# A second short GpSimd store ahead of the copies of zeros, and the copies cut 2, 9 and 4 instead of 11 and 4

## The chip, the core and the metric

The kernel runs on one core of one Trainium2 chip. The metric is the device time of one execution in microseconds; before the change it is 284.01 us, the median of four runs (283.77 to 284.34).

## What is computed

One decode step (one token for each of 4 batches) through a layer norm, attention over the last 1024 positions of a 4096 position cache, and a gelu-gated feed-forward block; then all gradients for a given `grad_out`. Cut to what matters here:

```python
def _A_ref(x, k_cache, v_cache, wq, wo):
    W = min(4096, max(256, Sk // 4))                       # 1024 of Sk = 4096
    k = jnp.repeat(k_cache[:, :, Sk - W:, :], rep, axis=1)
    v = jnp.repeat(v_cache[:, :, Sk - W:, :], rep, axis=1)
    ...
_out, _vjp = jax.vjp(_f, A_x, A_k_cache, A_v_cache, A_wq, A_wo, B_w_gate, B_w_up, B_w_down)
_grads = _vjp(grad_out)
```

The gradients of the two caches (`out_2` for K, `out_3` for V) have shape 4 x 8 x 4096 x 128 in bfloat16. Only the last 1024 of the 4096 rows of each head carry values. The first K0 = 3072 rows are zero, and must be written all the same: 2 x 4 x 8 x 3072 x 256 bytes, some 50 MB of the 81 MB that the kernel writes.

## The kernel before

The work goes through four steps `t` of two kv heads each; a feed-forward part stands in front. TensorE transposes and multiplies, VectorE and ScalarE take the results out of PSUM into staging tiles, and SyncE (SP) sends these to memory in the program's order. The stores of zeros are laid between these by hand: `zero()` (L161) sends two heads of one batch, 1536 KB, from the tile `ztile` as 128 pieces of 12288 bytes.

An execution's memory traffic is carried out by 16 DMA engines (not to be confused with the five compute engines). Each works through its share of every transfer, packet by packet, in the order of its queue; SP's transfers are one queue (q1), GpSimd's another (q0), ScalarE's a third (q10). In the trace each packet is a record with start, duration, size and queue, without the number of its engine. The end of an engine's share is a packet of 4 bytes, a completion mark.

`zero_15()` (L166) is called once, in the last step, and treats four heads of `out_3` in its own way. Head 3 is one store of SP (128 rows of 6144 bytes). For heads 0 to 2, GpSimd (POOL) copies from zeros that already lie in `out_2[0]`, memory to memory:

- L183, first, a short store: 5 rows of 16 positions each, that is 5 pieces of 4096 bytes from `ztile` to head 0.
- L184 to L186, two copies. With KR = K0 / 16 = 192, a "row" is 192 positions, 49152 bytes, for each of the 3 heads. The first copy has 11 such rows (33 pieces), the second 4 (12 pieces): 45 pieces, 15 x 192 = 2880 of the 3072 positions of each head.
- L187 and L188: what is left of heads 0 to 2 (192 positions less the 80 of the short store for head 0) goes out as three stores of 16 rows by SP, at the very end of the program, after head 3.

Each store is `store()` (L99, its transfer on L103), which also tells the scheduler that stores write disjoint parts. The order on each engine is that of the program. `zero_15()` is called after the products of the last softmax gradient are issued; on POOL its transfers stand behind the last two multiplications of L487.

Of the kernel before, what the change touches and what calls it, by code (L numbers as in the profile page):

```python
# [18 lines left out]
def kernel(  # L19
# [28 lines left out]
    nc = tc.nc  # L48
# [7 lines left out]
    K0 = Sk - W  # L56
# [43 lines left out]
    def store(eng, out, in_, kind):  # L100

        eng.nop()
        d = eng.dma_start(out=out, in_=in_)  # L103
        for k in ("rest", "zeros") if kind == "rest" else ("rest",):
            tc.declare_no_dep(d.ins, group=k, reason="stores write disjoint parts of the outputs")
        tc.add_to_no_dep_group(kind, d.ins)
        return d
# [58 lines left out]
    def zero_15():  # L166


        last = [z for z in zlist if z[0] is out_3][-2:]
        for z in last:  # L170
            zlist.remove(z)
        b, g = last[0][1:]
        assert last[1][1:] == (b, g + ZR)
        dst = out_3[b, g:g + 2 * ZR]
        KR = K0 // 16
        k0 = 15 * KR
        used = [80, 0, 0]

        def rest(eng, n, h, k0, w):
            src = ztile[0:8 * n - 7:8] if n < 16 else ztile[0:n]  # L180
            store(eng, dst[h, k0:k0 + n * w, :].rearrange("(m j) d -> m (j d)", m=n), src[:, 0:w * Dh], "zeros")

        rest(nc.gpsimd, 5, 0, k0, 16)  # L183
        for n, r in ((11, 0), (4, 11)):  # L184
            s_, d_ = (x[0:3, r * KR:(r + n) * KR, :].rearrange("g (m j) d -> m g (j d)", m=n) for x in (out_2[0], dst))
            store(nc.gpsimd, d_, s_, "zeros")  # L186
        return [lambda: rest(nc.sync, P, 3, 0, K0 // P)] + [  # L187
            lambda h=h: rest(nc.sync, 16, h, k0 + used[h], (KR - used[h]) // 16) for h in range(3)]  # L188


    nc.gpsimd.memset(ztile[:], 0.0)
# [512 lines left out]
    for f4 in range(NF4):  # L704
        held = {}
        n = min(4, NF - 4 * f4)
# [34 lines left out]
    with tc.tile_pool(name="kv_b", bufs=GP, reuse_waits="tile") as kv_b, \  # L741
# [7 lines left out]
        for t in range(NT):  # L749
# [13 lines left out]
            if t == NT - 1:  # L763
                rest = zero_15()
# [81 lines left out]
```

## Time and profile before

| | us |
|---|---|
| median of four runs | 284.01 |
| the profiled execution | 283.98 |
| its span in the trace | 282.2 |
| PE, DVE, ACT busy | 203.2, 164.4, 118.0 |
| POOL busy | 42.0 |
| last PE instruction ends | 255.6 |
| last DVE instruction ends | 260.6 |
| the three POOL transfers of `zero_15()` are issued | 224.37, 224.95, 225.57 |
| SP's last five transfers are issued | 265.82 to 271.38 |
| last packet on a DMA engine ends | 280.22 |

All times within the trace count from the start of the span. A row of the stretches view gives, for each stretch of time, the busy time of the engines, the granted clock of TensorE, the mean busy share of the 16 DMA engines and the rate that they moved. A row of the timeline gives start, duration, engine, line and what was moved.

### The profile page before, as it was taken

To read this page: it belongs to the slowest core of one execution; us is meant where nothing else is said; L and a number is where in the kernel's file an instruction comes from. 1 tells how busy PE (TensorE), PEld (TensorE's weight loads), DVE (VectorE), ACT (ScalarE), POOL (GpSimd) and SP (SyncE) were. 2 spreads that over 40 slices of the span, in tenths; PEclk is the share of its full clock that TensorE was granted. 3 is DMA by queue.
4 is the path that set the end of the run, shared out by engine and by line. 5 is a ranking of instruction groups with operands and counts; after the bars stand their busy time and mean duration, and the time that the engine had idled before them with its cause. 6 is when DMAs were issued, how large, how long until landed. Compare 5 with 4: busy or idle time off the path is not lost.

```text
span 282.2 us, 6863 instructions
## 1 busy us (share of the span) xinstructions
PE 203.2 (72%) x2962; PEld 139.5 (49%) x2972; DVE 164.4 (58%) x313; ACT 118.0 (42%) x219; POOL 42.0 (15%) x43
## 2 busy tenths in 40 slices
PE   0276699959789889998999199898999599272000
PEld 0265476735456675556765056676555474031000
DVE  7946646645776555577666158767677638178000
ACT  2030386635035418753547155453866048160000
POOL 8600000007002250002340000232000600000000
PEclk9999589986999999999999869999999979958555
DMA  7999999999999999999999999999999999999991
GB/s 269 392 376 432 429 423 419 428 422 419 368 398 425 410 409 420 425 403 422 423 413 414 420 428 422 423 387 410 380 370 413 398 383 377 411 428 426 412 419 44
DMA packets 19677, 112.12 MB, mean 397 GB/s; under 512 B 1806, under 2 KB 4654, under 8 KB 11411
## 3 DMA queue, kind: packets, MB, share of 16 engines
q1 hardware_dynamic: 17696, 101.33, 87.5%
q0 software_dynamic: 1792, 8.52, 7.7%
q10 hardware_dynamic: 160, 1.84, 1.8%
q8 instruction: 23, 0.38, 0.5%
q14 instruction: 6, 0.05, 0.0%
HBM read 32.89 MB, written 81.01 MB: 404 GB/s over the span
## 4 chain that ended last, share of the span: by engine, by line
PE 47%; DMA 23%; DVE 15%; ACT 3%; issue 2%; SPq 0%; DVEq 0%; ACTq 0%
DMA out_dram<-stg_dv 13%; PE T_ps L303 8%; PE kv_ps L508 6%; DMA wd_sb<-in_B_w_down_dram 6%; PE S_ps L369 5%; PE od_ps L474 5%; DMA out_dram<-osb_g 4%; DVE T_sb L98 3%; PE dwq_ps L544 2%; DVE dS_s L391 2%; PE wdT_ps L303 2%; PE acc_ps L280 2%; PE wgT_ps L303 2%; PE dwd_ps L684 2%; DVE P_s L391 2%
## 5 line engine op out<-in xcount | busy, mean ns | idle before, releaser
L98 DVE COPY T_sb<-T_ps 128x1024 bf16<-128x1024 bf16 x64 | 44.1, 689 | 26.9 <-PE T_ps L303 26.8
L97 ACT CAST stg_dk<-kv_ps 128x512 bf16<-128x512 f32 x52 | 29.2, 588 | 33.1 <-DMA out_dram<-stg_dv 13.4
L97 ACT CAST stg_dv<-kv_ps 128x512 bf16<-128x512 f32 x51 | 28.1, 588 | 25.1 <-PE kv_ps L508 24.5
L508 PE MATMUL kv_ps<-qmr,dS_s 128*128 128x512 bf16 x62 | 23.3, 412 | 13.1 <-ACT stg_dk L97 12.4
L487 POOL TENSOR_TENSOR o_s<-od_r,msk_r 128x512 bf16<-128x512 bf16 x8 | 9.1, 1159 | 110.4 <-DVE od_r L479 81.1
L303 PE MATMUL T_ps<-ident,vb 128*128 128x128 bf16 x256 | 20.5, 226 | 0.6 <-DVE T_sb L98 0.3
L303 PE MATMUL T_ps<-ident,kb 128*128 128x128 bf16 x256 | 20.6, 226 | 0.2 <-issue 0.2
L303 PEld LDWEIGHTS <-kb 128*128 128x128 bf16 x256 | 17.6, 102 | 4.5 <-issue 1.5
L303 PEld LDWEIGHTS <-vb 128*128 128x128 bf16 x256 | 17.4, 102 | 5.1 <-issue 3.2
L508 PE MATMUL kv_ps<-domr,P_s 128*128 128x512 bf16 x58 | 19.7, 382 | 0.1
L97 ACT CAST osb_q<-dwq_ps 128x512 bf16<-128x512 f32 x25 | 14.6, 586 | 8.8 <-PE dwq_ps L544 7.8
L353 POOL TENSOR_TENSOR domr<-r,msk 128x1024 bf16<-128x1024 bf16 x4 | 7.6, 1895 | 71.1 <-DVE r L350 65.0
L97 ACT CAST osb_g<-dwg_ps 128x512 bf16<-128x512 f32 (+1 forms) x25 | 12.4, 544 | 11.9 <-PE dwg_ps L697 4.5
L98 DVE CAST stg_dk<-kv_ps 128x512 bf16<-128x512 f32 x12 | 8.0, 689 | 13.8 <-DMA out_dram<-stg_dv 13.0
L97 ACT CAST osb_o<-dwo_ps 128x512 bf16<-128x512 f32 x24 | 13.8, 586 | 4.6 <-PE dwo_ps L529 3.6
L98 DVE COPY wgT<-wgT_ps 128x1024 bf16<-128x1024 bf16 x14 | 9.6, 687 | 6.9 <-PE wgT_ps L303 6.9
L508 PEld LDWEIGHTS <-dS_s 128*128 128x128 bf16 x64 | 6.2, 101 | 14.2 <-issue 13.1
L369 PE MATMUL S_ps<-T_sb,qm 128*32 128x256 bf16 x128 | 12.7, 388 | 0.6 <-DVE T_sb L98 0.5
L369 PE MATMUL S_ps<-T_sb,dom 128*32 128x256 bf16 x128 | 12.7, 388 | 0.1
L529 PE MATMUL dwo_ps<-dyr,o_s 128*128 128x512 bf16 x32 | 12.6, 420 | 0.3 <-ACT stg_dk L97 0.2
L98 DVE COPY woT<-woT_ps 128x1024 bf16<-128x1024 bf16 x16 | 11.0, 686 | 2.6 <-PE woT_ps L303 2.2
L544 PE MATMUL dwq_ps<-od_r,xnm 128*128 128x256 bf16 x64 | 12.0, 287 | 0.2 <-ACT osb_q L97 0.2
(190 smaller groups left out, 386.8 us busy)
## 6 DMA issues: line engine op xcount, KB each, us to landing
out_dram<-ztile SPq DMA_DIRECT2D x30, 1536.0 KB, 19.2
kb<-in_A_k_cache_dram SPq DMA_DIRECT2D x8, 1024.0 KB, 19.7
vb<-in_A_v_cache_dram SPq DMA_DIRECT2D x8, 1024.0 KB, 21.9
out_dram<-stg_dv SPq DMA_DIRECT2D x8, 1024.0 KB, 16.3
out_dram<-stg_dk SPq DMA_DIRECT2D x8, 1024.0 KB, 19.5
out_dram<-osb_o SPq DMA_DIRECT2D x8, 512.0 KB, 16.0
out_dram<-osb_q SPq DMA_DIRECT2D x8, 512.0 KB, 19.3
out_dram<-osb_g SPq DMA_DIRECT2D x8, 448.0 KB, 11.4
```

What stands on the lines that cost most here:

```text
L97: return nc.scalar.copy(out=out, in_=in_)
L98: return nc.vector.tensor_copy(out=out, in_=in_)
L280: nc.tensor.matmul(ps[:, c, :], lhsT=lf(c), rhs=rhs, start=(k == 0), stop=(k == len(terms) - 1))
L303: nc.tensor.transpose(ps[:, i, :], a, ident[:])
L353: nc.gpsimd.tensor_tensor(out=mr[:].rearrange("p g q d -> p (g q) d"), in0=r4[:, k, :].unsqueeze(1).broadcast_to([P, SL, Dh]), in1=msk[:]. ...
L369: nc.tensor.matmul(ps[b * RB:(b + 1) * RB, :], lhsT=zt[:, b * GP + g, c0:c0 + RB], rhs=T_sb[:].rearrange("p (x b) -> p b x", b=B)[:, b, :] ...
L391: nc.vector.scalar_tensor_tensor(out=out[:], in0=src[:].unsqueeze(2).broadcast_to([P, WQ, B]), scalar=rr[:, 0:1], in1=mskb[:].unsqueeze(1) ...
L474: nc.tensor.matmul(od_ps[g * 32:g * 32 + B * rep, k, g, :], lhsT=cols[:, jj, g * NQ + q, :], rhs=blks[(t, g)][:, j, :], start=(j == 0), st ...
L487: nc.gpsimd.tensor_tensor(out=o_s[:, g], in0=rows[:, g].unsqueeze(1).broadcast_to([P, rep, Dh]), in1=msk_r[:].unsqueeze(2).broadcast_to([P ...
L508: nc.tensor.matmul(mps[:].rearrange("p q d -> p (q d)"), lhsT=src[:, j * P:(j + 1) * P], rhs=mr[:, g].rearrange("p q d -> p (q d)"), start ...
L529: nc.tensor.matmul(mps[:], lhsT=o_s[:, g].rearrange("p r d -> p (r d)")[:, i:rep * Dh:rep], rhs=dyr[:], start=True, stop=True)
L544: nc.tensor.matmul(mps[:, i].rearrange("p g d -> p (g d)"), lhsT=xnm[:, i2 * 2 + i, c * P:(c + 1) * P], rhs=dq_r[:].rearrange("p g d -> p ...
```

## The change

`zero_15()` alone is changed. Ahead of the short store of 5 rows stands another, of 8 rows of 4096 bytes, to head 1. The copies become three: 2 rows of 160 positions (40960 bytes for each head), 9 rows of 192 and 4 rows of 192 (49152 bytes each). They cover 2 x 160 + 13 x 192 = 2816 positions of each head instead of 2880, so 256 positions of each head are left instead of 192; less the short stores (80 of head 0, 128 of head 1), the three stores of SP at the end have 16 rows of 11, 8 and 16 positions instead of 7, 12 and 12. On SP and the compute engines the order of instructions stays.

```diff
-        KR = K0 // 16
-        k0 = 15 * KR
-        used = [80, 0, 0]
+        rows = ((2, 160), (9, 192), (4, 192))
+        k0 = sum(n * w for n, w in rows)
+        used = [5 * 16, 8 * 16, 0]
...
+        rest(nc.gpsimd, 8, 1, k0, 16)
         rest(nc.gpsimd, 5, 0, k0, 16)
-        for n, r in ((11, 0), (4, 11)):
-            s_, d_ = (x[0:3, r * KR:(r + n) * KR, :].rearrange("g (m j) d -> m g (j d)", m=n) for x in (out_2[0], dst))
+        r0 = 0
+        for n, w in rows:
+            s_, d_ = (x[0:3, r0:r0 + n * w, :].rearrange("g (m j) d -> m g (j d)", m=n) for x in (out_2[0], dst))
             store(nc.gpsimd, d_, s_, "zeros")
+            r0 += n * w
         return [lambda: rest(nc.sync, P, 3, 0, K0 // P)] + [
-            lambda h=h: rest(nc.sync, 16, h, k0 + used[h], (KR - used[h]) // 16) for h in range(3)]
+            lambda h=h: rest(nc.sync, 16, h, k0 + used[h], (K0 - k0 - used[h]) // 16) for h in range(3)]
```

## The prediction, made before the result was known

> **What bounds the kernel now.** I read the page's slices first, then the last 12 us by stretches, then the queues of SP and POOL, and last the packet records.
>
> ```profile
> span 282.2 us, 6863 instructions
> ...
> PE   0276699959789889998999199898999599272000
> ...
> DMA  7999999999999999999999999999999999999991
> GB/s 269 392 376 432 429 423 419 428 422 419 368 398 425 410 409 420 425 403 422 423 413 414 420 428 422 423 387 410 380 370 413 398 383 377 411 428 426 412 419 44
> ```
>
> The reader is to see that TensorE stops three slices before the end (a slice is 7.06 us) while the DMA row stays at 9 until the last slice, which moves 44 GB/s after 419. Memory traffic sets the end. The chain of waits ends on VectorE at 260.6, twenty microseconds short, so it does not name the bound. The stretches of the end do:
>
> ```profile
> 273.30:275.40 2.10, 0.00 (x0) 0.00 (x0) 0.00 (x0) 0.00 (x0) 0.00 (x0) 0.50 0.91 377
> 275.40:276.40 1.00, 0.00 (x0) 0.00 (x0) 0.00 (x0) 0.00 (x0) 0.00 (x0) 0.50 0.36 137
> 276.40:277.30 0.90, 0.00 (x0) 0.00 (x0) 0.00 (x0) 0.00 (x0) 0.00 (x0) 0.50 0.12 50
> 277.30:280.20 2.90, 0.00 (x0) 0.00 (x0) 0.00 (x0) 0.00 (x0) 0.00 (x0) 0.50 0.06 24
> 280.20:282.20 2.00, 0.00 (x0) 0.00 (x0) 0.00 (x0) 0.00 (x0) 0.00 (x0) 0.50 0.00 0
> ```
>
> The last two columns are the busy share of the 16 DMA engines and GB/s. From 277.3 to 280.2 the share is 0.06, that is 1/16: **one DMA engine works alone for 2.9 us**, and two before that (0.12). I followed packet records backwards from each of the 16 last completion marks, joining a packet to the one that begins within a few ns of its end and keeping to the known order of transfers. The 16 engines end at 273.32, thirteen of them from 275.31 to 276.34, 277.34 and 280.22. All get the same bytes from SP. So the question of this change is what it does to the **late engine** of 280.22.
>
> It is not late because of POOL's copies; it was behind before them. SP issued the two stores of `osb_q` (2048-byte packets, 16 for each engine) at 216.71 and 219.48, and most engines have done both by 221. The transfers view for a later stretch:
>
> ```profile
> DMA packets 140, 1.18 MB, mean 408 GB/s; under 512 B 17, under 2 KB 17, under 8 KB 49
> ```
>
> This is 223.9 to 226.8; 49 less 17 leaves 32 packets of 2048 bytes, both stores of one engine, one after the other, while all else is 12288-byte zeros. From 226.95 to 280.22 that engine's records leave no idle gap: what is taken off it shortens the end one for one, until 277.34 is reached. Engines with a lead do idle (the earliest for 0.53 us at 262.86 and 0.99 us at 266.2, waiting for SP's next transfer).
>
> **Who carries what.** POOL's transfers now:
>
> ```profile
> 224.37 0.58 POOL L103 DMA_DIRECT2D out_dram<-ztile  x1
> 224.95 1.27 POOL L103 DMA_DIRECT2D out_dram<-out_dram  x2
> ```
>
> The pieces in q0: five of 4096 bytes start at 229.22, 229.53, 229.59, 229.70, 229.84, taking 179, 305, 794, 448 and 159 ns. In all five chains one completion mark, at most one 12288-byte packet or two follow, then a 49152-byte piece. Six other chains show two marks and then such pieces; four show six marks first; one shows marks alone. So 11 engines carry the 11-row copy (3 pieces each), 4 others the 4-row copy, one nothing, and **the five engines of the short store are among the eleven**. The short store thus did not push the copy on to other engines: both begin at the same place. The late engine is one of the five (its chain: 4096 bytes at 229.70, pieces from 230.85, 233.27, 235.15). The 1024-byte rows of `out_b` and `dx_b`, which go to four engines, appear in four chains with a short row and never in the late one. If the four are neighbours, the late engine stands at one end of the five: first or last.
>
> **The change part by part.**
>
> 1. *Copy of 2 rows of 160 in place of the first two of the eleven.* The first two engines get 3 x 40960 instead of 3 x 49152 bytes. An undisturbed 49152-byte piece takes 1.815 us (27 of the 45 are below 1.9), so a sixth of it three times is 0.91 us; by the late engine's own pieces (2.0, 1.88, 1.87 us) 0.96. If the late engine is the first: -0.91. If it is the last: 0. Both ends are kept. I take **first**: when the program starts, the four engines of the 4-row load of `x` begin at 1.75 to 1.81, fifteen engines have their first 14336-byte packet by 2.59 and one only at 3.26; if engines start in their order, a last one stands just ahead of the first of the next round. This is thin, and the chances say so.
> 2. *Short store of 8 rows.* One row more for the first eight engines, the late one in either case: 0.159 us undisturbed, up to 0.794 by the dearest of the five. I take 0.16, the shortest row, since the late engine's other packets of that time were only some 8% above their usual length.
> 3. *Two transfers more on POOL.* Two issues by 0.58 and 0.62 us: the 2-row copy is issued 0.58 us later, the 9- and 4-row copies 1.2 us later. Nothing is behind them on POOL but the end. The late engine has SP's zeros to do meanwhile (packets up to 239), so it pays nothing. The other engines have little from SP between 231 and 233.81, when SP issues the next store, and would do up to 1.2 us of copying later: 277.34 becomes at most 278.5, still hidden behind the late engine's 279.5. If that cover were gone, this would be the bound. The 4-row copy waits for a POOL transfer of before 160 us, long landed. Two more completion marks of 9 ns: 0.02.
> 4. *SP's last stores* change from 7, 12, 12 to 11, 8, 16 positions, 1024 bytes more for each engine. Their packets took 74 + 121 + 121 ns; at the same rate 0.04 us more. Same issues, same waits, so nothing else on SP.
>
> Sum on the late engine: -0.91 + 0.16 + 0.02 + 0.04 = **-0.69 us**; its end 280.22 becomes 279.53. The 2.0 us from there to the end of the span, and the 1.73 from span to time, stay. 283.98 - 0.69 = 283.29; the profiled execution is 0.03 below the median, so **283.3 us**.
>
> The Trainium skill ("DMA: Bandwidth & Descriptors", "Why a DMA increments its semaphore by 16 and not by 1") has GpSimd transfers on fewer than 16 engines take consecutive engines from a cursor that goes round. The five chains speak against a cursor moved by the 5-row store. Were it moved by the new 8-row store, the light rows would be eight engines further on, the late engine would keep its 48 KB, and the sum would be about 284.0 to 284.2.
>
> The same page ("Latency and other measured facts") says that engines 7 and 15 are usually slower. This trace shows one such engine and no number; if it is 15, and the four engines of 4-row transfers are 0 to 3, then the late engine is the first of the five and the sum above holds.
>
> **Rivals.**
>
> - *The light rows miss the late engine* (it is the last of the five, or the 8-row store moves the start). Then only +0.16 + 0.02 + 0.04: 284.2. For it: nothing in the trace numbers the engines. Against: the start order. Chance 0.37.
> - *The copies' places shift so far that the late engine gets none.* It would lose 3 x 1.815 = 5.4 us and end near 275; the engine now without copies, 273.32 less 1.5 us of idling plus 5.4, ends by 277.3, and 277.34 sets the end: -2.9, 281.1. Against: it needs a shift by exactly the right number. Chance 0.04.
> - *Slower.* The light rows miss, and the added short row meets the crowd at 229 to 230 us, where a 4096-byte packet took 794 ns: +0.79, with the marks, the last stores and a little more delay of its first piece +0.9: 284.9. It decides from a row of 0.51 us on (0.57 us is 0.2%, less 0.06). Two of the five rows were at or near that. Chance 0.11.
>
> **Numbers.** The forecast has 0.48, and of it a fifth may come out within 0.2% of 284.01 (between 283.44 and 284.58, about what a measurement of this kernel can tell from no change). Faster: 0.48 x 0.8 + 0.04, some 0.43. Same: 0.37 + 0.10 less a little for a dear row, 0.44. Slower 0.13. The range goes from 282.9 (light rows at the late engine's own prices and the 8-row store hidden) over the first rival to 284.5, leaving out the two outer cases. Alone, the forecast's own range is 283.0 to 283.6.
>
> **What would show it.** In the changed trace: the late engine's three pieces are of 40960 bytes and its last mark is near 279.5, with a stretch of share 0.06 of some 2 us ahead of it; eight rows of 4096 and then five, all in chains that go on with copies. Three pieces of 49152 in the late chain mean the first rival; no pieces, the second. Wrong altogether would be a last engine that had been among the thirteen, or a hole between 231 and 234 that makes SP's stores late.

## The result: 0.65 us slower

The changed kernel takes 284.92 us, the median of 38 runs (283.95 to 286.6), beside 284.19 us for 63 runs of before (283.6 to 285.53). The ratio is 1.0023, 95% interval 1.0016 to 1.0031: **slower by 0.65 us** (0.45 to 0.88), where 283.3 and a gain of 0.7 had been forecast. The profiled execution took 284.97 us (before: 283.98). Its page, in the rows that were read of before:

```profile
span 283.3 us, 6865 instructions
...
PE   0275699969888889988999099898999599082000
...
DMA  7999999999999999999999999999999998999990
GB/s 268 392 376 429 432 424 420 421 420 414 363 390 427 413 417 424 426 419 426 412 404 412 426 427 422 425 402 411 386 368 406 409 413 317 414 427 426 407 393 26
```

TensorE again stops three slices ahead of the end, and the DMA row is full up to it: the kind of bound has not changed. The stretches of the end (times, busy time of the engines, clock, then busy share of the 16 DMA engines and GB/s):

```profile
275.40:276.40 1.00, 0.00 (x0) 0.00 (x0) 0.00 (x0) 0.00 (x0) 0.00 (x0) 0.50 0.58 230
276.40:277.30 0.90, 0.00 (x0) 0.00 (x0) 0.00 (x0) 0.00 (x0) 0.00 (x0) 0.50 0.13 52
277.30:280.20 2.90, 0.00 (x0) 0.00 (x0) 0.00 (x0) 0.00 (x0) 0.00 (x0) 0.50 0.06 23
280.20:281.30 1.10, 0.00 (x0) 0.00 (x0) 0.00 (x0) 0.00 (x0) 0.00 (x0) 0.50 0.06 25
281.30:283.30 2.00, 0.00 (x0) 0.00 (x0) 0.00 (x0) 0.00 (x0) 0.00 (x0) 0.50 0.00 0
```

The share of 0.06, one engine of 16 at work alone, now lasts until 281.3 instead of 280.2. By the packets the 16 engines end at 274.02, fourteen of them from 275.12 to 276.92, and the late one at 281.31. The engine that ended second at 277.34 before is now hidden by more than four us. So the whole loss is on the late engine: +1.09 us in these two executions.

That it is the same engine shows in the stretch from 223.9 to 226.8:

```profile
DMA packets 141, 1.20 MB, mean 414 GB/s; under 512 B 17, under 2 KB 17, under 8 KB 49
```

49 less 17 is 32 again: both stores of `osb_q` on one engine, long after the others. POOL's issues:

```profile
224.04 1.16 POOL L103 DMA_DIRECT2D out_dram<-ztile  x2
225.19 1.88 POOL L103 DMA_DIRECT2D out_dram<-out_dram  x3
```

Two more issues, 1.2 us, as expected. Followed from its end backwards, the late engine has a row of each short store (192 and 165 ns), then some nine marks, then three pieces of **49152** bytes at 234.99, 237.62 and 240.16. That fits the last copy alone, the 4-row one. Before, its pieces were in the first copy and had begun by 230.85. The late engine got no light row, and its pieces run four us later:

| late engine, us | before | changed | changed, another profile |
|---|---|---|---|
| begins SP's zeros behind `osb_q` at | 226.79 | 226.99 | 227.00 |
| ends | 280.22 | 281.31 | 281.40 |
| between the two | 53.43 | 54.32 | 54.40 |
| its three pieces together | 5.7 | 6.5 | 6.6 |
| its short rows together | 0.45 | 0.36 | 0.33 |
| excess over undisturbed lengths, up to 230 | 0.7 | 0.4 | 0.4 |
| the same, from 230 on | 0.8 | 1.8 | 1.9 |

Undisturbed lengths are the commonest ones of the traces: 12288 bytes 457 ns, 49152 bytes 1815 ns, and so on; a packet counts to the start of the next. The last column is the profile of a repeat (below). The third row is the cleaner measure, since the first lies ahead of everything that the change touches. It tells 0.9 to 1.0 us, of which 0.16 is the second short row and 0.04 SP's last stores; the rest, some 0.7, is packets that took longer. Which of the five short rows of before is the late engine's is not certain: the records join about as well through the row of 0.79 us as through the one of 0.45 us. The rows on the excess do not depend on it much, since they count what a short row took beyond its 0.16 as well.

### The profile page after: what moved, and what is told of

Same layout as the page of the kernel before. It is cut to its first block, busy times and chain, and to the rows that moved or that the text cites. A ratio compares the mean times of both kernels' runs of the same rounds, so it can differ in the third digit from the quotient of the medians.

```text
span 283.3 us, 6865 instructions
## 1 busy us (share of the span) xinstructions
PE 202.7 (72%) x2962; PEld 139.6 (49%) x2972; DVE 164.2 (58%) x313; ACT 117.7 (42%) x219; POOL 43.2 (15%) x45
## 4 chain that ended last, share of the span: by engine, by line
DMA 43%; PE 32%; DVE 11%; ACT 4%; issue 2%; SPq 0%; DVEq 0%; ACTq 0%
DMA out_dram<-stg_dv 22%; DMA out_dram<-osb_o 9%; PE T_ps L306 6%; DMA wd_sb<-in_B_w_down_dram 6%; PE kv_ps L511 4%; PE S_ps L372 4%; DMA out_dram<-osb_g 4%; PE od_ps L477 4%; DMA out_dram<-osb_d 3%; PE dwq_ps L547 2%; DVE T_sb L98 2%; PE wdT_ps L306 2%; PE acc_ps L283 1%; DVE P_s L394 1%; PE dwo_ps L532 1%
```

## The experiments

The working assumption after the comparison was a **model of places**. Number the DMA engines by where the copies of before start: the first copy takes places 1 to 11, the second 12 to 15, and 16 gets nothing. A copy takes as many places as it has rows, and the next goes on behind it. The 8-row store moves the start by 8, the 5-row one does not. The late engine is place **five**. Then, in the changed kernel, the light rows are on 9 and 10, the 9-row copy on 11 to 16 and 1 to 3, the 4-row copy on 4 to 7, and place 8 has nothing. The main rivals: the late engine is not fixed, some engine is always late; or rows and orders by themselves cost the time.

All diffs are against the changed kernel. Times are medians; "before" is measured beside each group, on the same chip. Differences in us are worked out from the ratio.

| run | us | before | ratio (95%) | difference |
|---|---|---|---|---|
| e1_no8 | 285.31 | 284.55 | 1.0030 (1.0012 to 1.0047) | +0.85 |
| e2_shift_only | 284.94 | 284.55 | 1.0014 (0.9991 to 1.0036) | +0.40 |
| e3_skip_late | 284.74 | 284.55 | 1.0002 (0.9981 to 1.0023) | +0.06 |
| e4_light_late | 283.90 | 284.55 | 0.9983 (0.9965 to 1.0002) | -0.48 |
| e5_four_first | 284.36 | 284.52 | 0.9993 (0.9980 to 1.0006) | -0.20 |
| **e6_tiny_copy** | **281.33** | 284.52 | **0.9875** (0.9855 to 0.9894) | **-3.56** |
| e7_two_fives | 284.62 | 284.52 | 1.0012 (0.9994 to 1.0030) | +0.34 |
| e8_no5 | 284.70 | 284.52 | 1.0004 (0.9989 to 1.0019) | +0.11 |
| e9_no_short | 284.18 | 284.28 | 1.0001 (0.9989 to 1.0013) | +0.03 |
| e10_three_fives | 284.56 | 284.28 | 1.0015 (1.0003 to 1.0027) | +0.43 |
| e11_nine_first | 284.15 | 284.28 | 0.9996 (0.9987 to 1.0005) | -0.11 |
| e12_changed | 284.85 | 284.28 | 1.0024 (1.0009 to 1.0039) | +0.68 |
| e13_thirteen_first | 285.21 | 284.61 | 1.0022 (1.0005 to 1.0039) | +0.63 |
| e14_third_copy | 285.38 | 284.61 | 1.0031 (1.0014 to 1.0049) | +0.88 |
| e15_no5_again | 284.73 | 284.61 | 1.0005 (0.9989 to 1.0020) | +0.14 |
| e16_no8_again | 284.60 | 284.61 | 1.0018 (1.0000 to 1.0037) | +0.51 |
| e17_tiny_four | 284.25 | 284.78 | 0.9984 (0.9961 to 1.0007) | -0.46 |
| e18_tiny_six | 284.74 | 284.78 | 1.0003 (0.9987 to 1.0019) | +0.09 |

### Which engine is late, and is it one?

**e4_light_late**: the 4-row copy first, then the light one.

```diff
-        rows = ((2, 160), (9, 192), (4, 192))
+        rows = ((4, 192), (2, 160), (9, 192))
-        used = [5 * 16, 8 * 16, 0]
+        used = [5 * 16, 0, 0]
...
-        rest(nc.gpsimd, 8, 1, k0, 16)
```

> The 5-row store alone, then copies of 4 rows of 192, 2 rows of 160 and 9 rows of 192. Place theory with a late engine that is the fifth from the start: it gets three pieces of 40960 bytes, -0.9 us from the bytes, less up to 0.5 if its pieces start later in the queue: 283.3 to 283.8. If it is the first from the start, as the prediction took it: no change from the bytes. Number theory: +0.35 us.

Measured: 283.90, -0.48 us (the interval just takes in no change). The late engine's three pieces are of 40960 bytes, at 232.40, 234.50 and 236.68, and it ends at 279.75. The light copy is on places 5 and 6 here; in the chains of before the late engine was one of the five, at one end of them. So it is the fifth. The end in the trace:

```profile
276.40:277.70 1.30, 0.00 (x0) 0.00 (x0) 0.00 (x0) 0.00 (x0) 0.00 (x0) 0.50 0.29 100
277.70:279.70 2.00, 0.00 (x0) 0.00 (x0) 0.00 (x0) 0.00 (x0) 0.00 (x0) 0.50 0.06 24
279.70:281.80 2.10, 0.00 (x0) 0.00 (x0) 0.00 (x0) 0.00 (x0) 0.00 (x0) 0.50 0.00 0
```

The stretch with one engine is 2.0 us, as the forecast had it for the changed kernel: its mechanism was right, at another place.

**e3_skip_late**, a miss: it was to leave the late engine without pieces, by short stores of 4 rows and 1.

```diff
-        rows = ((2, 160), (9, 192), (4, 192))
+        rows = ((11, 192), (4, 192))
-        used = [5 * 16, 8 * 16, 0]
+        used = [4 * 16, 1 * 16, 0]
...
-        rest(nc.gpsimd, 8, 1, k0, 16)
-        rest(nc.gpsimd, 5, 0, k0, 16)
+        rest(nc.gpsimd, 4, 0, k0, 16)
+        rest(nc.gpsimd, 1, 1, k0, 16)
```

> Copies cut 11 and 4 as before, but short stores of 4 rows and of 1 row in place of the 5-row store. Place theory, with a late engine that is the fifth from the start, and short stores of 1, 4 and 8 rows that move the start while one of 5 does not: the copies begin five engines on, the late engine gets none, its end falls by 5.4 us and the next one, near 277.3, sets the end: -2.9 us, some 281.3, ratio 0.990. If stores of 4 and 1 do not move the start, or the late engine is the first of the five: within 0.3 us of before. Number theory: +0.35 us.

Measured: +0.06 us. The store of one row went out as 16 pieces of 256 bytes on all engines, and chains with a 4096-byte row of the 4-row store went on directly with the 11-row copy: neither store moved the start. The late engine has no 4096-byte row, which agrees with place five, and three pieces of 49152 bytes. It says that these stores don't move a start, and nothing of what a gap on the late engine is worth.

**e6_tiny_copy**: the same aim with a copy instead of a store, since copies had moved the start each time.

```diff
-        rows = ((2, 160), (9, 192), (4, 192))
+        rows = ((5, 16), (11, 192), (4, 192))
-        used = [5 * 16, 8 * 16, 0]
+        used = [0, 0, 0]
...
-        rest(nc.gpsimd, 8, 1, k0, 16)
-        rest(nc.gpsimd, 5, 0, k0, 16)
```

> Both short stores are gone; the copies have 5 rows of 16 positions (4096-byte pieces), 11 and 4 rows of 192. A transfer between memories moved the start of the next by its rows in every run so far, so the five tiny rows take the first five engines, the late engine (the fifth) among them, and the 11 and 4 rows the other eleven and the first four. Theory (one engine, the fifth, sets the end, and what it carries counts one for one): it loses three pieces of 49152 bytes, 5.7 us, and is done near 274.5; the second engine of before, 277.3, sets the end: some 2.9 us faster than before. Rival (the end is a matter of all the traffic, and some engine is always late): within 0.5 us of before, with another engine alone at the end.

Measured: **281.33 us** (5 runs, 280.29 to 281.40), 3.2 us less than before by the medians and 3.56 (3.0 to 4.1) by the ratio. It beats both kernels. The page and the stretches of its end:

```profile
span 279.6 us, 6863 instructions
...
DMA  7999999999999999999999999999999999999995
```

```profile
273.30:275.20 1.90, 0.00 (x0) 0.00 (x0) 0.00 (x0) 0.00 (x0) 0.00 (x0) 0.50 0.96 404
275.20:276.40 1.20, 0.00 (x0) 0.00 (x0) 0.00 (x0) 0.00 (x0) 0.00 (x0) 0.50 0.81 329
276.40:277.60 1.20, 0.00 (x0) 0.00 (x0) 0.00 (x0) 0.00 (x0) 0.00 (x0) 0.50 0.28 112
277.60:279.60 2.00, 0.00 (x0) 0.00 (x0) 0.00 (x0) 0.00 (x0) 0.00 (x0) 0.50 0.00 0
```

No stretch with a share of 0.06 is left: all engines end between 275.21 and 277.57. The late engine is now the **first** to end, at 275.21, with three pieces of 4096 bytes at 229.83, 230.46 and 231.12 and no other. The rival, that some engine is always late, falls.

**e17_tiny_four** and **e18_tiny_six**: the same with one tiny row less, and one more.

```diff
-        rows = ((2, 160), (9, 192), (4, 192))
+        rows = ((4, 16), (11, 192), (4, 192))
-        used = [5 * 16, 8 * 16, 0]
+        used = [0, 0, 0]
...
-        rest(nc.gpsimd, 8, 1, k0, 16)
-        rest(nc.gpsimd, 5, 0, k0, 16)
```

and the same with `(6, 16)`.

> As the run with a tiny copy of 5 rows, but of 4 rows. If a copy moves the start by its rows and the late engine is the fifth, the engine left without large pieces is now the fourth, an ordinary one, and the late engine is the first of the 11-row copy again: within 0.3 us of before. If the gain of 3.2 us came from something else (no short stores, a copy of small pieces first): about -3 us here too.

> The same with 6 tiny rows: the engine left without large pieces is the sixth; the late engine gets three tiny pieces and, in the last copy, three of 49152 bytes. Theory: +0.3 to +0.9 us against before (three tiny pieces, and a late place for the large ones). If the gain came from something else than the engine left out: about -3 us.

Measured: -0.46 (no change within its interval) and +0.09 us. In both the gain of e6_tiny_copy is gone, to within half a microsecond. The end of e17_tiny_four, then of e18_tiny_six:

```profile
275.40:277.20 1.80, 0.00 (x0) 0.00 (x0) 0.00 (x0) 0.00 (x0) 0.00 (x0) 0.50 0.50 183
277.20:280.40 3.20, 0.00 (x0) 0.00 (x0) 0.00 (x0) 0.00 (x0) 0.00 (x0) 0.50 0.06 25
```

```profile
275.40:277.70 2.30, 0.00 (x0) 0.00 (x0) 0.00 (x0) 0.00 (x0) 0.00 (x0) 0.50 0.41 164
277.70:280.70 3.00, 0.00 (x0) 0.00 (x0) 0.00 (x0) 0.00 (x0) 0.00 (x0) 0.50 0.06 26
```

One engine works alone for 3 us again in both. The tiny pieces bear it out: with four rows all twelve take 159 ns; with five, the late engine's three take 159, 201 and 173 ns and the other twelve 159; with six, three take 164, 220 and 176 ns and the other fifteen 159. The late engine is among the first five and not among the first four. For e18_tiny_six +0.3 or more had been expected, for a late place of the large pieces; that part did not come.

### What the move and the rows cost

**e12_changed** is the changed kernel once more, without an edit.

> The changed kernel once more, to stand beside these three. As measured so far: +0.65 us against before (0.45 to 0.88).

Measured: +0.68 us. The loss is real, and its trace gives the third column of the table above.

**e2_shift_only**: both short stores, and the copies of before.

```diff
-        rows = ((2, 160), (9, 192), (4, 192))
+        rows = ((11, 192), (4, 192))
```

> Only the 8-row store is added; the copies stay cut 11 and 4 with 49152-byte pieces. Place theory: as the changed kernel, +0.7 us, ratio 1.002 to 1.003, and the late engine's three pieces are issued with the 4-row copy. Number theory: +0.35 us. Cut theory: no change.

Measured: +0.40, too wide to tell from nothing. The trace shows the move: the engine without copies has one 4096-byte row, that of the 8-row store, where in before it had none. With a row of this store and none of the 5-row store, which takes five of the same places, the empty place is the sixth, seventh or eighth: the 8-row store moves the start by 6, 7 or 8, and e13_thirteen_first below leaves 8.

**e1_no8** and, repeated, **e16_no8_again**: the 5-row store alone. **e11_nine_first**: the same with the 9-row copy ahead of the light one. By the model the late engine is in the second copy in the first two, and in the first copy in the third.

```diff
-        used = [5 * 16, 8 * 16, 0]
+        used = [5 * 16, 0, 0]
...
-        rest(nc.gpsimd, 8, 1, k0, 16)
```

and, for e11_nine_first, in addition:

```diff
-        rows = ((2, 160), (9, 192), (4, 192))
+        rows = ((9, 192), (2, 160), (4, 192))
```

> Only the 8-row store is left out; the copies stay cut 2, 9 and 4 and SP's last stores 11, 16 and 16 positions. Place theory (the 8-row store moves the start of the copies on by 8 engines, which puts the late engine into the last copy; without it the copies begin where they began before): time as before, ratio 0.998 to 1.001. Number theory (each transfer more on GpSimd delays the copies): half of the change, some +0.35 us. Cut theory (the sizes of the pieces or SP's last stores cost): all of the change, +0.7 us.

> The changed kernel without its 8-row store once more (late engine in the second of three copies, one short row, 0.1 us more at the end). First measured at +0.85 us, while the same with the 9-row copy first was at -0.1. If place is the cause: +0.4 us or more again. If the first measurement was off: +0.1 to +0.2 us.

> As the run without the 8-row store, but the 9-row copy is issued ahead of the 2-row one, so that the late engine stands in the first copy, as before, with three pieces of 49152 bytes and one short row. Against before only SP's last stores differ for it (11, 16 and 16 positions, 0.1 us more). If the 0.8 us that the run without the 8-row store lost came from being in the second copy: +0.1 us against before. If it came from what both have, the copies cut in three and the larger stores at the end: +0.6 to +0.9 us.

Measured: +0.85, then +0.51 (0.0 to 1.05), then -0.11. The late engine has 49152-byte pieces in all three, at 232.22, 231.29 and 229.79: without the 8-row store the light rows miss it as well. That undoing this one store does not bring the gain back shows that the move is not the only reason; the fifth is not the first. Being in the second copy seems to cost something, but:

**e5_four_first**: the copies of before with the 4-row one ahead, so that the late engine is in the second copy with nothing else changed.

```diff
-        rows = ((2, 160), (9, 192), (4, 192))
+        rows = ((4, 192), (11, 192))
-        used = [5 * 16, 8 * 16, 0]
+        used = [5 * 16, 0, 0]
...
-        rest(nc.gpsimd, 8, 1, k0, 16)
```

> Short store of 5 rows, then the 4-row copy ahead of the 11-row one. No bytes change on any engine but the one without copies; the late engine, fifth from the start, is the first of the 11-row copy, which is now issued second, about 0.6 us later. Theory (in the changed kernel its three pieces cost 0.8 us more because they were in the last copy and ran 4 to 5 us later, beside more traffic): +0.3 to +0.8 us against before, with pieces that start after 231.5 and last more than 5.8 us in sum. Rival (place in the queue is nothing): within 0.2 us of before, pieces of 5.7 us in sum.

Measured: -0.20 (-0.57 to +0.17), against the theory, although the pieces did run later (232.19) and take longer (6.20 us together).

**e14_third_copy**: as e5_four_first, with `rows = ((2, 192), (2, 192), (11, 192))`.

> The kernel before with its copies cut in 2, 2 and 11 rows of 192: the late engine stays in the 11-row copy, but that is now issued third. Same bytes, same single short row, same last stores, eight marks ahead of its pieces. If place makes the changed kernel slower: +0.3 to +0.6 us against before. If place is nothing: within 0.2 us.

Measured: +0.88. Its late engine has pieces at 233.99, 236.48 and 238.83 (2.04, 1.88, 2.58 us). But here the whole 11-row copy is late, and the 45 pieces took 2.22 us in the mean, against 2.01 before; it is more than one engine's place that changed.

**e8_no5** and **e15_no5_again**: the 8-row store alone, the late engine in the last copy with one short row.

```diff
-        used = [5 * 16, 8 * 16, 0]
+        used = [0, 8 * 16, 0]
...
-        rest(nc.gpsimd, 5, 0, k0, 16)
```

> The changed kernel without its 5-row store: the 8-row store, then copies of 2, 9 and 4 rows. The late engine keeps one short row (of the 8-row store), and the copies start 8 engines on, so that it stands in the 4-row copy, issued last. Theory (place): as the changed kernel, +0.5 to +0.8 us against before. Rival (the second short row): about 0.5 us less than that, +0.0 to +0.2. Rival (the 8-row store moves the start only together with the 5-row one): the late engine in the 9-row copy, as in the run without the 8-row store.

> The changed kernel without its 5-row store once more (late engine in the last copy, one short row). If place makes the changed kernel slower: +0.4 to +0.6 us. If the second short row does: +0.1 us, as the first measurement had it.

Measured: +0.11 and +0.14. The pieces start at 233.20 and 233.64, in the last copy, and take 5.78 and 5.91 us together. The move and the last place alone are not what costs 0.65.

**e13_thirteen_first**: both short stores, 13 rows in the first copy, then the light one.

```diff
-        rows = ((2, 160), (9, 192), (4, 192))
+        rows = ((13, 192), (2, 160))
```

> The changed kernel's two short stores, then 13 rows of 192 positions in one copy and the 2 rows of 160 after it. The copies start 8 engines on, so the late engine is the thirteenth place: in the first copy, not the last. It has the same two short rows, the same bytes and the same last stores as in the changed kernel; only its place is earlier. If place makes the changed kernel slower: +0.2 to +0.3 us against before (second short row and last stores). If the rows do: as the changed kernel, +0.65 us.

Measured: +0.63, as the changed kernel, with pieces from 232.26. So the last place is not needed either, with the two rows kept. The pieces are of 49152 bytes; had the 8-row store moved the start by 6 or 7, the light rows would have reached the fifth place here. That leaves 8.

**e9_no_short**, **e7_two_fives**, **e10_three_fives**: none, two and three short stores of 5 rows on the copies of before. Nothing moves; the late engine has 0, 2 and 3 short rows where before it has 1. The edit of the last:

```diff
-        rows = ((2, 160), (9, 192), (4, 192))
+        rows = ((11, 192), (4, 192))
-        used = [5 * 16, 8 * 16, 0]
+        used = [5 * 16, 5 * 16, 5 * 16]
...
-        rest(nc.gpsimd, 8, 1, k0, 16)
         rest(nc.gpsimd, 5, 0, k0, 16)
+        rest(nc.gpsimd, 5, 1, k0, 16)
+        rest(nc.gpsimd, 5, 2, k0, 16)
```

> The kernel before without its short store (SP's last three stores carry 12, 12 and 12 positions instead of 7, 12 and 12): no row of 4096 bytes on the late engine, 0.05 us more at the end, nothing moved. If a short row is cheap, as the prediction had it (0.16): -0.1 us against before. If a row costs what the late engine's own took in the crowd (0.45 to 0.8): -0.4 to -0.75 us. If a short store is of use for something else (it holds the copies back): slower than before.

> Two short stores of 5 rows, to heads 0 and 1, ahead of the copies of 11 and 4 rows as before. Five-row stores did not move the start of the copies, so nothing moves: the late engine gets a second short row, and stays in the first copy. Theory that place costs the time and the row little: +0.2 us at most (0.16 for the row, 0.02 for marks, less 0.04 at the end). Rival (the second short row is what made the changed kernel slower): +0.6 to +0.8 us, with a row of over 0.5 us on the late engine.

> The kernel before with three short stores of 5 rows, one for each of the heads 0, 1 and 2 (SP's last stores carry 7, 7 and 7 positions): two rows more on the late engine, 0.1 us less at the end, the copies at the same places. Cheap row: +0.2 us against before. Dear row: +0.8 to +1.5 us.

Measured: +0.03, +0.34 and +0.43. Two rows more cost 0.43, and 0.1 was saved by SP's smaller last stores: some 0.26 us for a row (0.1 to 0.4 by the interval). Leaving out the only row gained nothing that can be told (-0.3 to +0.4). In the traces the late engine's rows are cheap, 201 and 174 ns with two stores, 160, 182 and 174 ns with three.

## Why the prediction was wrong

- **The bound** was right. One engine's queue sets the end, in every trace in which it has large pieces, and what it carries counts nearly one for one: without its pieces 3.2 to 3.6 us were gained, somewhat more than the 2.9 that the trace of before had up to the second engine. The price of the rival in which the late engine gets no copies, 281.1, and 277.3 as the next bound were right too: 281.33 and 277.57 in e6_tiny_copy.
- **Five of the eleven, the late engine at one end of them**: right. **"I take first" is the step that failed.** It rested on the order in which engines start at the program's beginning, fifteen by 2.59 us and one at 3.26. That says that one engine is late, not which place it has. The late engine is the fifth (e4_light_late, and 4, 5 and 6 tiny rows), so the term of -0.91 us was 0. Apart from this hint the evidence in hand left the two ends even.
- **The 8-row store does not move the start** was inferred from the 5-row store, and failed as well: it moves it by 8. It did not decide, since without that store the light rows miss too (e1_no8, e16_no8_again, e11_nine_first).
- **The second short row, +0.16**: 0.26 with a wide interval, and 0.16 to 0.19 in the trace of the changed kernel. The late engine's own row of before, which the prediction put at 229.70 us, is not certain (see the table of the result). The rival that priced it at 0.79 was close to the measured time by its sum, and not by its cause.
- **Two more POOL transfers, 0**: the other engines hide them, as said (276.92, not 278.5). For the late engine "it pays nothing" is the second step that failed: its pieces came four us later, and took 6.5 us instead of 5.7. With the row and SP's last stores the sum is 0.22 (0.16, 0.02, 0.04), the 284.2 of the first rival; measured is +0.65. The other 0.4 appears in the traces as longer packets on the late engine from 230 us on (excess 1.8 and 1.9, before 0.8; ahead of 230 it was before that lost more, 0.7 against 0.4). The stretches of that time, of before and then of the changed kernel:

```profile
231.00:233.80 2.80, 2.80 (x29) 1.70 (x26) 2.45 (x5) 2.45 (x6) 0.00 (x0) 1.00 0.91 320
233.80:236.00 2.20, 2.11 (x38) 1.35 (x37) 1.62 (x4) 1.22 (x3) 0.00 (x0) 1.00 0.84 346
236.00:239.00 3.00, 2.73 (x11) 0.87 (x10) 2.81 (x6) 2.86 (x6) 0.00 (x0) 1.00 0.90 380
```

```profile
231.00:233.80 2.80, 2.73 (x33) 1.67 (x32) 2.46 (x5) 2.62 (x5) 0.00 (x0) 1.00 1.27 433
233.80:236.00 2.20, 2.17 (x33) 1.15 (x32) 1.62 (x4) 1.24 (x3) 0.00 (x0) 1.00 1.01 346
236.00:239.00 3.00, 2.73 (x11) 0.95 (x10) 2.81 (x6) 2.86 (x6) 0.00 (x0) 1.00 0.93 325
```

From 233.8 to 236 the engines move the same 346 GB/s for a busy share of 1.01 instead of 0.84, and from 236 to 239 only 325 for 0.93: a byte takes longer, and the late engine is in the middle of its pieces. That the one comes of the other is argued and not shown: in e8_no5 and e15_no5_again the pieces were in the last copy too, and took 5.78 and 5.91 us instead of 6.5.

**What stays open** is what of the change makes them longer. The rows alone (some 0.26), the last place alone (+0.1, twice), and the second copy (-0.20 in one form, +0.85 and +0.51 in another) do not add up to one rule, and with differences of 0.3 to 0.5 us, intervals of about 0.5 us either way don't allow one to be chosen.

The cursor of which the Trainium skill tells ("DMA: Bandwidth & Descriptors", "Why a DMA increments its semaphore by 16 and not by 1") is borne out for the copies and for the store of 8 rows. The same section has an exception, by which GpSimd spreads some direct copies over all 16 engines, with the number of rows divided by 16 and rounded up on each, so that 100 rows put data on engines 0 to 14. The 5-row store behaves like such a copy: it leaves the cursor where it is, and it does not begin there either. In the changed kernel the cursor stands at place 9 when the 5-row store comes, so at the cursor its rows would lie on places 9 to 13; but the late engine, place five, has a row of both stores (192 and 165 ns), and so has at least one other engine (rows at 229.06 and 229.85). The 4-row store left the cursor where it was as well. Why a store of 8 rows goes by the cursor and these do not, no run shows.

The page's engines 7 and 15 ("Latency and other measured facts") do not help here: if place 1 is engine 0, as the exception would have it, the late one is engine 4. The traces give places, and no numbers.

## What to carry to other kernels

When one DMA engine is alone at work at the end, find its place before the shares are weighted: an edit that takes the pieces off one place after another (here a tiny copy of 4, 5 and 6 rows) shows it at once, 284.25, 281.33 and 284.74 us. Weighting a neighbour is worth nothing, and what is added in front still has to be paid for. Take the whole share off the late engine rather than a sixth of it, as long as the next engine's end leaves room.

## What the runs showed of the hardware that was not expected

- Whether a short GpSimd store moves the engine on which the next transfer starts depends on its rows: stores of 8 rows moved it by 8, stores of 5, 4 and 1 rows not at all, and copies in memory moved it by their rows. The 5-row store did not follow a moved start either: behind the 8-row store its rows shared engines with that store's. A store of one row of 4096 bytes was cut into 16 pieces of 256.
- One engine ended alone, 2.2 to 4.5 us behind the next, in every trace in which it had large pieces, and in all of those where its place could be read it was the fifth. Its 4096-byte pieces took 159 to 220 ns where the others took 159 in the same copies.
- A memory-to-memory piece of 49152 bytes took 1.815 us undisturbed and up to 3.5 us in the crowd of 231 to 240 us (e2_shift_only, at 232.73).
